# Two 1 KB reads of k and v put ahead of the first loads of a fused attention and channel-mix kernel

## The chip, the cores and the metric

The kernel runs on one core of one Trainium2 chip. The metric is the device time of one execution in microseconds (us). Unless a run says otherwise, a time is the median of its runs, with the lowest and highest behind it. The program uses a single core, so it has no second, slower die to compare against; the runs counted as fast are those within 1.5% of the fastest of the same kernel, and all comparisons use those.

## The reference

Eight batches of 8 heads, 576 positions, 64 features per head. A linear attention, then a channel mix whose input is the attention's output:

```python
def _attn_ref(q, k, v):
    q_s = np.exp(q - max over the last axis);  q_s = q_s / sum over the last axis
    k_s = np.exp(k - max over positions);      k_s = k_s / sum over positions
    kv = np.einsum('bhsd,bhse->bhde', k_s, v)
    return np.einsum('bhsd,bhde->bhse', q_s, kv)

def _moe_ref(x, mu_k, mu_r, w_k, w_v, w_r):
    xk = mu_k * x + (1.0 - mu_k) * x_prev        # x_prev: x one position earlier
    xr = mu_r * x + (1.0 - mu_r) * x_prev
    k = np.maximum(xk @ w_k, 0.0)
    return 1.0 / (1.0 + np.exp(-(xr @ w_r))) * (k * k @ w_v)
```

(Shortened: the maxima and sums are written in words, and the guards of 1e-09 and the casts are left out.)

## The kernel before

The kernel plans its instructions in advance: each operation is added to a plan with an engine, a cost and a key, and a scheduler emits them in the order of their planned start. What matters here is how batch 0 gets in. Six loads, q, k and v of head group 0 and then of group 1, each in two halves of 288 KB, fill the buffers raw_a to raw_f. The first load is issued by ACT, the other five by SP:

```python
PARTS = {1: [slice(0, 2)], 2: [slice(0, 1), slice(1, 2)]}
FIRST = ((0, 0, ("ACT", "ACT")), (0, 1, ("SP", "SP")), (0, 2, ("SP", "SP")),
         (1, 0, ("SP", "SP")), (1, 1, ("SP", "SP")), (1, 2, ("SP", "SP")))
# ... (cut)
        def emit(engine, u):
            ap = bass.AP(tensor=src.tensor,
                         offset=src.offset + (b * H + 2 * g + 4 * u.start) * S * D,
                         ap=[[J * D, 128], [4 * S * D, u.stop - u.start], [1, J * D]])
            return queues[engine].dma_start(out=raws[slot.index][:, u, :], in_=ap)
```

So raw_a is q of group 0, raw_b k, raw_c v, and raw_d, raw_e, raw_f the same of group 1. Two small loads of the mixing vectors stand ahead of SP's five:

```python
    def emit_mu_rows_load():
        for m, src in enumerate((moe_mu_k, moe_mu_r)):
            nc.sync.dma_start(out=mu_rows[:, m, :], in_=bass.AP(
                tensor=src.tensor, offset=src.offset, ap=[[256, 2], [1, 256]]))
# ... (cut)
    for op in plan.order():
        op.made = op.emit()
        if op.engine == "POOL" and op.size and gate:
            tc.add_manual_dep(op.made.ins, gate.pop().made.ins.name, sync)
```

ACT takes the exponential of q and k (eq_a, ek_a for group 0, eq_b, ek_b for group 1), POOL casts v of group 0 (vv_a) and then issues the later loads and the weights (wk, wr, wv). The built program gives the DMAs of SP and ACT eight semaphores (counters that a landing raises) in turn: in the trace of the kernel before, the first halves of raw_a and raw_d, the first and the ninth DMA, share one. A ninth DMA is held on its queue until the first has landed; this is invisible in the source and is what most of this document is about. "The turn" below is a DMA's place in this round of eight.

The softmax here doesn't subtract the row's maximum and nothing guards it: scores larger than these inputs give would overflow.

Of the kernel before, what the change touches and what calls it, by code (L numbers as in the profile page):

```python
# [12 lines left out]
F32 = mybir.dt.float32  # L13
# [195 lines left out]
def kernel(  # L209
# [14 lines left out]
    B, H, S, D = q.shape  # L224
# [16 lines left out]
    plan = Plan(pools, shared)  # L241

    const = ctx.enter_context(tc.tile_pool(name="const", bufs=1))
# [47 lines left out]
    pick = const.tile([2, 2, 64], F32, name="pick")  # L291
    mu_all = const.tile([128, 2, 2, 2, 128], F32, name="mu_all")
    warm = const.tile([1, 1], F32, name="warm")



    copies = {"ACT": nc.scalar.copy, "DVE": nc.vector.tensor_copy, "POOL": nc.gpsimd.tensor_copy}
    queues = {"SP": nc.sync, "ACT": nc.scalar, "POOL": nc.gpsimd}
# [44 lines left out]
    def emit_late_consts():  # L343
        for t in xbs:
            nc.vector.memset(t[:, :, 0:1], 0.0)

    zero = plan.add("DVE", 0.1, 0.15, -10, emit_warm_zero)
    plan.add("ACT", 1.55, 1.6, 3.5, emit_warm, [zero])
    identity = plan.add("POOL", 0.6, 0.8, -9.1, emit_identity)
# [74 lines left out]
    for h in range(2):  # L424
        wv_done.append(plan.add("POOL", 0.8, 0.8, LOADS.index(f"wv{h}"), lambda h=h: emit_wv(h), gate,
                                size=1200.0))
# [434 lines left out]
```

## Time and profile before

| | before |
|---|---|
| time, first three runs | 202.3 us (201.98 to 202.84) |
| span of the profiled execution | 200.2 us, clock 0.997 |
| raw_d's first half issued, landed | 3.63, 9.54 us |
| first half of eq_b starts | 9.56 us |
| first dense matmul with a record | 18.30 us (the record of the one before it is missing; its weight load starts at 17.88) |

The prediction below shows the busy line, the chain of waits and some short windows. The timeline of SP's queue in the kernel before (columns: start us, length us, engine, line, operation, output<-input, count):

```profile
1.46 0.83 SPq L310 DMA_DIRECT2D raw_b<-in_k_dram  x2
2.33 0.90 SPq L310 DMA_DIRECT2D raw_c<-in_v_dram  x2
3.63 0.82 SPq L310 DMA_DIRECT2D raw_d<-in_q_dram  x2
4.49 1.57 SPq L310 DMA_DIRECT2D raw_e<-in_k_dram  x2
```

raw_b and raw_c go out back to back. Between the end of raw_c's issue (3.23) and raw_d's there are 0.40 us with nothing: the ninth DMA waits for the first half of raw_a. The Trainium skill, "Perfetto Trace Analysis", section "DMA Instruction — HWDGE (DVE, Sync)", says that the start of such an instruction in a profile is the moment when its semaphores are satisfied, and that the movement of the data is not in its length. The trace agrees on both: raw_d's issue starts at 3.63, 0.02 us after raw_a landed, lasts 0.82 for two halves, and the data land 5.91 us after it.

The second view is a table of windows of the kernel before (window, length, five engines' busy time with counts, clock, DMA share, GB/s; a packet counts whole in the window in which it starts):

```profile
3.60:5.20 1.60, 1.28 (x2) 0.50 (x2) 0.85 (x2) 1.36 (x2) 0.00 (x0) 1.00 0.96 313
5.20:6.40 1.20, 0.76 (x1) 0.00 (x0) 1.20 (x4) 0.94 (x2) 0.00 (x0) 1.00 0.91 255
6.40:7.60 1.20, 0.37 (x10) 0.24 (x14) 1.03 (x2) 0.46 (x2) 0.89 (x1) 1.00 1.03 359
7.60:8.80 1.20, 0.58 (x36) 0.45 (x36) 0.00 (x0) 0.44 (x1) 1.13 (x3) 1.00 1.01 388
```

### The profile page before, as it was taken

The numbers are of one execution on the slowest core, as the hardware profiler recorded it, in microseconds if no ns is written. First come the engines' busy times: TensorE is split into PE (matmuls) and PEld (weight loads), VectorE is DVE, ScalarE is ACT, GpSimd is POOL, SyncE is SP. The second block draws the span as 40 slices with busy tenths as digits, with TensorE's granted clock in tenths as the row PEclk, the third lists the DMA queues.
The fourth block names the chain that finished last, engine by engine and source line by source line (L and its number), as shares of the span: only waits on it lengthen the run. The fifth ranks groups of instructions, "written<-read, shape, count | busy, mean of one in ns | idle before, by whom it ended". The sixth has DMA issues, their size and how long they took to land.

```text
span 200.2 us, 5314 instructions
## 1 busy us (share of the span) xinstructions
PE 183.6 (92%) x2147; PEld 96.6 (48%) x2171; DVE 160.6 (80%) x348; ACT 136.9 (68%) x212; POOL 40.7 (20%) x66
## 2 busy tenths in 40 slices
PE   2547999999999999999999999999999999999992
PEld 0234554545444555454476455455455544544761
DVE  2498469798999999999979999999998998432531
ACT  5494595998999799978559978946842662552440
POOL 1584365644354123411300000000000000000000
PEclk9999999999999999999999999999999999999998
DMA  6999999999999999993991220242042204402514
GB/s 196 348 277 227 281 256 352 391 398 412 388 403 405 403 405 362 398 378 110 262 365 47 54 56 0 52 111 51 3 100 62 52 3 105 105 0 54 118 41 105
DMA packets 15520, 40.72 MB, mean 203 GB/s; under 512 B 2300, under 2 KB 3592, under 8 KB 15496
## 3 DMA queue, kind: packets, MB, share of 16 engines
q0 software_dynamic: 7840, 27.40, 40.6%
q1 hardware_dynamic: 7208, 12.26, 21.4%
q10 hardware_dynamic: 448, 0.72, 1.2%
q8 instruction: 17, 0.28, 0.6%
q14 instruction: 7, 0.06, 0.1%
HBM read 33.56 MB, written 9.44 MB: 215 GB/s over the span
## 4 chain that ended last, share of the span: by engine, by line
PE 88%; DMA 4%; DVE 3%; issue 1%; ACT 1%; DVEq 0%
PE mm_c L766 10%; PE mm_a L722 10%; PE mm_d L722 9%; PE mm_d L766 8%; PE mm_a L766 7%; PE mm_c L722 7%; PE mm_b L766 6%; PE mm_b L722 6%; PE mm_b L756 6%; PE mm_d L756 4%; PE mm_c L756 3%; PE att_b L520 3%; PE mm_a L756 3%; DMA raw_d<-in_q_dram 3%; PE att_a L520 3%; PE att_b L507 2%
## 5 line engine op out<-in xcount | busy, mean ns | idle before, releaser
L722 PEld LDWEIGHTS <-wk 128*128 128x128 bf16 x320 | 35.4, 114 | 27.7 <-issue 2.2
L722 PE MATMUL mm_a<-xk,wk 128*128 128x512 bf16 (+1 forms) x96 | 24.2, 362 | 0.3 <-issue 0.2
L722 PE MATMUL mm_d<-xk,wk 128*128 128x512 bf16 (+1 forms) x87 | 22.4, 370 | 0.1
L766 PEld LDWEIGHTS <-k_b 128*128 128x128 bf16 x152 | 14.5, 98 | 15.7 <-issue 0.7
L756 PEld LDWEIGHTS <-xr 128*128 128x128 bf16 x144 | 13.9, 98 | 15.9
L766 PEld LDWEIGHTS <-k_a 128*128 128x128 bf16 x144 | 13.4, 97 | 15.5 <-issue 0.4
L722 PE MATMUL mm_c<-xk,wk 128*128 128x512 bf16 (+1 forms) x66 | 16.0, 358 | 0.4 <-issue 0.3
L722 PE MATMUL mm_b<-xk,wk 128*128 128x512 bf16 (+1 forms) x62 | 15.5, 352 | 0.2
L756 PE MATMUL mm_b<-wr_bf,xr 128*128 128x512 bf16 x50 | 13.3, 379 | 0.1
L766 PE MATMUL mm_c<-wv_bf,k_a 128*128 128x512 bf16 x46 | 12.1, 379 | 0.2 <-issue 0.2
L766 PE MATMUL mm_c<-wv_bf,k_b 128*128 128x512 bf16 x47 | 12.1, 379 | 0.2 <-issue 0.2
L761 ACT ACTIVATE th_a<-mm_b 128x512 f32<-128x512 f32 x12 | 7.1, 595 | 6.4 <-PE mm_b L756 4.9
L766 PE MATMUL mm_d<-wv_bf,k_b 128*128 128x512 bf16 x39 | 10.1, 379 | 0.2 <-issue 0.2
L766 PE MATMUL mm_b<-wv_bf,k_a 128*128 128x512 bf16 x38 | 10.0, 379 | 0.2 <-issue 0.2
L766 PE MATMUL mm_a<-wv_bf,k_b 128*128 128x512 bf16 (+1 forms) x39 | 9.4, 358 | 0.1
L756 PE MATMUL mm_d<-wr_bf,xr 128*128 128x512 bf16 x34 | 9.1, 379 | 0.1
L766 PE MATMUL mm_d<-wv_bf,k_a 128*128 128x512 bf16 x28 | 7.5, 379 | 0.4 <-issue 0.3
L710 DVE TENSOR_TENSOR k_a<-rel_b 128x512 bf16<-128x512 bf16 (+1 forms) x14 | 5.6, 398 | 2.8 <-ACT rel_b L706 2.8
L710 DVE TENSOR_TENSOR k_a<-rel_c 128x512 bf16<-128x512 bf16 (+1 forms) x13 | 5.1, 389 | 3.4 <-ACT rel_c L706 3.4
L761 ACT ACTIVATE th_b<-mm_c 128x512 f32<-128x512 f32 x6 | 3.7, 610 | 5.6 <-PE mm_c L756 4.7
L756 PE MATMUL mm_c<-wr_bf,xr 128*128 128x512 bf16 x28 | 7.2, 379 | 0.1
L756 PE MATMUL mm_a<-wr_bf,xr 128*128 128x512 bf16 x28 | 7.2, 379 | 0.0
(275 smaller groups left out, 416.7 us busy)
## 6 DMA issues: line engine op xcount, KB each, us to landing
out_dram<-ot_a SPq DMA_DIRECT2D x24, 128.0 KB, 3.8
out_dram<-ot_b SPq DMA_DIRECT2D x24, 128.0 KB, 3.0
out_dram<-ot_c SPq DMA_DIRECT2D x22, 128.0 KB, 2.8
raw_b<-in_k_dram POOLq DMA_DIRECT2D x3, 576.0 KB, 9.4
raw_c<-in_v_dram POOLq DMA_DIRECT2D x3, 576.0 KB, 8.9
raw_d<-in_q_dram POOLq DMA_DIRECT2D x3, 576.0 KB, 10.1
raw_a<-in_q_dram POOLq DMA_DIRECT2D x2, 576.0 KB, 10.5
raw_e<-in_k_dram POOLq DMA_DIRECT2D x2, 576.0 KB, 11.6
```

Source lines behind the costliest of these rows:

```text
L507: nc.tensor.transpose(out=transposed()[64 * u:64 * u + 64, hf, 64 * j:64 * j + 64], in_=qss[qs.index][r, j, 64 * u:64 * u + 64], identity= ...
L520: nc.tensor.matmul(bank(xp)[64 * hf:64 * hf + 64, u, at + c:at + e], lhsT=w[r, hf, :], rhs=qts[qt.index][r, hf, src:src + e - c], start=(n ...
L710: nc.vector.tensor_tensor(out=k2s[k2.index][:, fc, 0:n], in0=rels[rel.index][:, 0:n], in1=rels[rel.index][:, 0:n], op=ALU.mult)
L722: nc.tensor.matmul(bank(kf)[:, 0:n], lhsT=(w[:, h, u, fc % 4:F // 2:4] if split[ct // 2] else w[:, u, F // 2 * h + fc % 4:F // 2 * (h + 1) ...
L756: nc.tensor.matmul(bank(rps), lhsT=xs[1][:, ct, c:c + 128], rhs=wr_bf[:, ct // 2 + 2 * (ct % 2), :], start=(ct == 0), stop=(ct == CT - 1))
L761: nc.scalar.activation(out=ths[th.index][:], in_=bank(rps), func=ACT.Tanh, scale=0.5)
L766: nc.tensor.matmul(bank(vps)[:, 0:w], lhsT=k2s[k2.index][:, ft, 128 * m:128 * m + 128], rhs=wv_bf[:, ft, e:e + w], start=(ft == 0), stop=( ...
```

## The change

The intent: the first read of k and of v by each DMA engine is taken to be slow, and v's falls bare on the path at 4.5 to 6.4 us. Two reads of 16 rows of 64 bytes each, spread over all 16 engines, should pay that price early, while the queue is still ramping up. The data are never used.

```diff
+    touched = const.tile([16, 5, 16], F32, name="touched")
# ... (cut)
+    def touch(engine, i, src, step):
+
+        return queues[engine].dma_start(out=touched[:, i, :], in_=bass.AP(
+            tensor=src.tensor, offset=src.offset, ap=[[step, 16], [1, 16]]))
+
+    for i, src in enumerate((k, v)):
+        plan.add("SP", 0.36, 0.4, i - 700, lambda i=i, src=src: touch("SP", i, src, 8 * S),
+                 size=10.0)
     zero = plan.add("DVE", 0.1, 0.15, -10, emit_warm_zero)
```

PE, DVE and ACT keep their order to the instruction. On POOL the first half of vv_a moves ahead of two small products.

## The prediction

> **What bounds the kernel now.** I read the busy line and the slices of the page first, then the chain of waits, then a table of short windows over the start, then the SP queue's timeline.
>
> ```profile
> PE 183.6 (92%) x2147; PEld 96.6 (48%) x2171; DVE 160.6 (80%) x348; ACT 136.9 (68%) x212; POOL 40.7 (20%) x66
> ...
> PE   2547999999999999999999999999999999999992
> ...
> DMA  6999999999999999993991220242042204402514
> ...
> PE 88%; DMA 4%; DVE 3%; issue 1%; ACT 1%; DVEq 0%
> ```
>
> TensorE is busy 183.6 of 200.2 us and is at 90% or more in every slice from the fifth to the last but one. Each slice is 5 us. What it lacks lies in the first four slices (about 20 us) and in the last. In windows of 20 us PE is busy 9.74 us of the first 20, between 19.50 and 19.89 of each later 20 and 16.11 of the last 20.2. So the middle is set by TensorE and the engines that feed it, and a change of the start is worth only as much as it moves the first dense matmuls (first layer, 18.30 us) earlier.
>
> The chain of waits at the start (columns: start us, us, what):
>
> ```profile
> 0.74 2.87 DMA raw_a<-in_q_dram
> 3.61 0.02 issue
> 3.63 5.91 DMA raw_d<-in_q_dram
> 9.54 0.02 issue
> 9.56 0.69 ACT eq_b L454
> 10.25 0.02 issue
> 10.27 1.50 DVE rsum_b L467 x2
> ...
> 13.41 0.69 PE att_b L507 x27
> ```
>
> The end is reached through raw_d, the q of batch 0's second group: ACT waits for it until 9.54 us, DVE sums and scales, PE transposes at 13.41. The step from raw_a to raw_d at 3.61 is a queue wait, not data: the built program gives SP's and ACT's DMAs eight semaphores in turn, and a ninth DMA waits until the first has landed. raw_d, the ninth, waits for raw_a's first half. But what sets 9.54 is bandwidth: six half loads of 288 KB (q, k, v in halves) are ahead of raw_d's first half. So the question is how fast the DMA engines run from 1.7 to 9.5 us. Windows of 0.2 us (columns: window, length, five engines' busy time, clock, DMA share, GB/s):
>
> ```profile
> 4.20:4.40 0.20, 0.20 (x1) 0.18 (x1) 0.05 (x1) 0.13 (x2) 0.00 (x0) 1.00 0.99 380
> ...
> 4.60:4.80 0.20, 0.20 (x1) 0.00 (x0) 0.20 (x1) 0.20 (x1) 0.00 (x0) 1.00 0.77 196
> 4.80:5.00 0.20, 0.20 (x2) 0.00 (x0) 0.20 (x1) 0.20 (x1) 0.00 (x0) 1.00 0.86 207
> ...
> 5.40:5.60 0.20, 0.20 (x1) 0.00 (x0) 0.20 (x1) 0.14 (x1) 0.00 (x0) 1.00 0.65 161
> ...
> 6.40:6.60 0.20, 0.00 (x0) 0.00 (x0) 0.20 (x1) 0.20 (x1) 0.00 (x0) 1.00 0.98 369
> ```
>
> The engines count as busy and move half as much from 4.6 to 5.8 us. The packets say why: a 2304-byte packet normally takes 93 ns, but from 4.5 to 6.4 some 35 of them took between 200 and 1148 ns. The same is seen from 1.7 to 2.9, where raw_a's first packets took up to 715 ns; the first mu packet took 838. At 3.6, where k's first packets are recorded, there is one of 918 and otherwise 93. The slow stretch at 4.6 comes just where the first engines end k's first half and may reach ahead to v. My reading, an inference: an engine's first access to a tensor is slow; q's is bare, k's was made early behind raw_a's traffic and is mostly hidden, v's stands bare on the path. That is what the change aims at.
>
> **What the Trainium skill says.** "DMA: Bandwidth & Descriptors", section "Why a DMA increments its semaphore by 16 and not by 1": the number of engines is the largest divisor up to 16 of the slowest dimension on both sides, so a touch of 16 rows uses all 16. The two mu loads have two rows, and the trace shows only two late steps of each one's semaphore, which agrees. The same page, "Latency and other measured facts", puts a tiny transfer's HBM round trip at about 800 ns at least; the mu packet's 838 ns agrees. The same page, "Issuing engines are not separate DMA queues", says that DMAs from SP and ACT share the 16 engines; in the window 3.0 to 4.4 the trace has ACT's queue at 57% and SP's at 46% of the engines' time, which agrees. No page that I found gives a price for an engine's first access to a tensor, so that price comes from the trace alone.
>
> **The change part by part.** I compared the instruction order of the two built kernels. PE, DVE and ACT keep theirs to the instruction.
>
> *Added:* two issues at the head of SP's queue. SP's two mu issues start 0.43 and 0.29 us before what follows (0.74, 1.17, 1.46), so two more of that kind move everything behind them on SP by about 0.7 us at most: the mu loads to about 1.46 and 1.75, raw_b from 1.46 to about 2.1. The mu row matmul at 3.92 moves to perhaps 4.5; ACT's copy of it at 6.05 stands behind ek_a, so this costs nothing, or a tenth or two on an engine that then waits anyway.
>
> raw_b's data are not wanted before raw_a's are through: its first packet is recorded at 3.5 us, and issued at 2.1 it can begin at about 3.1 (raw_a needed 1.0 us from issue to first packet). Cost about 0. The bytes, 2 KB at some 390 GB/s, are nothing.
>
> *Moved, semaphores:* two more DMAs turn the ring of eight by two. raw_c, not raw_d, is now the load that waits for raw_a's first half, so it is issued at about 3.65 rather than 2.33, and raw_d about 0.85 later than now, at about 4.5. At 3.65 raw_a and raw_b, 1.18 MB together, are not through: by 4.4 us the trace has moved 0.82 MB. raw_c's first packet can start at about 4.7, and the 1.18 MB end at about 5.3, so there are 0.6 us to spare. Cost about 0, with little room.
>
> *Removed:* the bare stall. From 4.4 to 6.0 the engines moved 0.39 MB, 242 GB/s by the page's count; at 390 they would have moved 0.62. The missing 0.23 MB are 0.6 us; the ragged recovery to 6.4 adds 0.1 to 0.2. At most 0.8 us.
>
> *Given back at the start:* the touches' own first accesses now fall with raw_a's, 16 engines times two tensors, when the engines ramp up (68, 127, 115, 196, 300, 362 GB/s in windows of 0.2 us from 1.6). The slow packets there end one after another, some 20 in 0.9 us. If accesses are served so, raw_a may land 0.1 to 0.4 us later. I take 0.2.
>
> *Moved, POOL:* vv_a's first half is cast ahead of mu_all's two products (1.36 us together), not behind. Its second half, now ending at 9.49, may end near 10.1, and the load raw_g, issued at 10.58 after raw_d's second half, comes at about 10.2: still not later than now.
>
> *Sum:* raw_d lands 0.8 - 0.2 = 0.6 us earlier, at 8.9. Behind it ACT, DVE and PE are chains of fixed length up to 18.30. The weights follow: the last of wk's rows landed at 21.70 for a matmul at 22.76, 1.06 us of slack, and POOL's issues move about 0.4 earlier too. So most of the 0.6 us is kept, and I take 0.55 off 202.3: **201.75 us**, which I round to 201.7.
>
> **The rivals.** *First: the touch does nothing.* If the slow packets at 4.6 are not first accesses to v but traffic between queues, or the price goes by smaller pieces of a tensor than the 288 KB which the touch's rows span (they step 18 KB), the stall stays. For it: the slow packets fall among k's second half as well, 590 KB into k, and v's own packets are not marked. Against it: raw_e and raw_f, later and from untouched parts of the same k and v, run at 369 to 449 GB/s from 9.4 to 11.2 us. It would give 202.3 to 202.6. *Second: the stall only moves* ahead onto raw_a, and raw_c's new semaphore wait runs the queue dry. For it: the serial look of the ends at 1.9 to 2.9 and only 0.6 us to spare. It would give 202.2 to 202.8. *Third: more is gained than the stall*, because engines no longer drift apart (raw_d's semaphore steps are spread from 8.18 to 9.54 over engines) and all land near the earliest. This gives up to 1.2 us, about 201.1. *Fourth: POOL becomes the gate,* raw_g and the weights come no earlier, and the gain is cut to about 0.4: 201.9.
>
> **Range and chances.** Three runs of the kernel before span 0.86 us, so noise alone makes about 0.4 either way. The working case is 201.75, the third rival 201.1, the first two 202.3 to 202.8: I set 200.9 to 202.5. Two per cent is 4 us. The whole start up to raw_d is 9.5 us and the stall in it 0.8, so faster by over 2% would need a second gain five times the stall; slower would need a queue that hangs for 4 us. Each gets 0.01.
>
> **What will show it.** Right: the windows from 4.6 to 6.4 stay above 350 GB/s; raw_d's wait in the chain ends near 8.9 instead of 9.54, and the transposes of att_b and the first dense matmul move by 0.4 to 0.6 us; PE's 183.6 us stay. The ramp of the first windows after 1.6 us is slower than now if the price was moved there. Wrong: the dip at 4.6 is still there (first rival); a gap in SP's queue opens after 5 us and raw_a lands later (second); raw_d lands at 8.9 but the dense matmuls still start at 18.3 (POOL or the weights gate it). The size will be wrong if TensorE's slow first matmuls, 616 to 634 ns at 18.3 to 20.8 against 379 later, fall otherwise.

## The result, and the profile after

| | before | after |
|---|---|---|
| time, same rounds | 202.34 us (201.98 to 202.84, 4 runs) | 203.19 us (202.93 to 203.27, 4 runs) |
| ratio after / before | | 1.0038 [1.0015, 1.0062] |
| span of the profiled execution | 200.2 us | 201.5 us, clock 0.994 |

A ratio here and below is the mean time of one kernel's fast runs over the mean of the other's of the same rounds, with its 95% interval, so it is not quite the ratio of the medians quoted. By the 2% measure the kernels are the same. But the change is slower by 0.4%, where the prediction had it 0.3% faster, and 203.19 lies outside its range. The changed kernel was later measured twice more, five rounds each, beside new runs of the kernel before: 1.0081 and 1.0079.

The page of the changed kernel: busy line, two rows of slices of about 5 us, and the chain by engine:

```profile
PE 185.6 (92%) x2171; PEld 96.6 (48%) x2171; DVE 160.6 (80%) x348; ACT 136.8 (68%) x212; POOL 40.0 (20%) x66
...
PE   0538999999999999999989999999999999999991
...
DMA  5999999999999999993892220242042204402514
...
PE 84%; DMA 8%; DVE 4%; SPq 1%; ACT 0%; issue 0%; DVEq 0%
```

The 185.6 us of PE against 183.6 before are no extra work: the line counts 2171 matmuls against 2147, while both kernels have 2171 weight loads, so 24 records were missing in the trace before. What these lines show of the difference is at the start: the first slices read 0538 where they read 2547, and "SPq", the queue of SP, has come into the chain. The first dense weight load starts at 18.67 us, 0.79 later than before.

SP's queue in the changed kernel:

```profile
0.74 0.40 SPq L350 DMA_DIRECT2D touched<-in_k_dram  x1
1.20 0.41 SPq L350 DMA_DIRECT2D touched<-in_v_dram  x1
...
2.28 0.83 SPq L311 DMA_DIRECT2D raw_b<-in_k_dram  x2
3.73 0.80 SPq L311 DMA_DIRECT2D raw_c<-in_v_dram  x2
4.58 0.91 SPq L311 DMA_DIRECT2D raw_d<-in_q_dram  x2
5.53 1.22 SPq L311 DMA_DIRECT2D raw_e<-in_k_dram  x2
```

raw_b goes out 0.82 us later than before (2.28 for 1.46), raw_c 1.40 later (3.73 for 2.33), raw_d 0.95 later (4.58 for 3.63). Between raw_b and raw_c SP stands still for 0.62 us. The chain says what for (start us, us, what):

```profile
0.74 2.97 DMA raw_a<-in_q_dram
...
3.73 0.33 SPq L311
...
4.10 0.43 SPq L311
...
4.58 5.72 DMA raw_d<-in_q_dram
...
10.32 0.69 ACT eq_b L463
```

raw_a lands at 3.71, SP issues raw_c's two halves at 3.73 and 4.10, and only then raw_d, which lands at 10.30. Everything behind raw_d is as long as before: eq_b starts 0.76 us later than in the kernel before (10.32 for 9.56), its second half 0.79 later, and so do the instructions of ACT up to 20.9 us.

What the DMA engines did meanwhile, in the same windows as shown of before:

```profile
3.60:5.20 1.60, 0.65 (x1) 0.50 (x2) 0.75 (x2) 1.36 (x2) 0.00 (x0) 1.00 0.86 160
5.20:6.40 1.20, 1.20 (x2) 0.00 (x0) 1.20 (x5) 0.00 (x0) 0.00 (x0) 1.00 0.92 353
6.40:7.60 1.20, 0.52 (x7) 0.20 (x10) 1.07 (x2) 1.18 (x3) 0.00 (x0) 1.00 1.01 357
7.60:8.80 1.20, 0.62 (x34) 0.49 (x35) 0.00 (x0) 0.56 (x1) 0.00 (x0) 1.00 0.89 244
```

Multiply each last column by its length. From 3.6 to 5.2 us the changed kernel moved 160 x 1.6 = 256 KB where 313 x 1.6 = 501 were moved before, 245 KB less. From 5.2 to 6.4 it moved 118 KB more: the dip of before is gone from this place. From 6.4 to 7.6 both are equal. From 7.6 to 8.8 it moved 173 KB less, a second dip. The balance is 300 KB, at the 390 GB/s of an undisturbed stretch 0.77 us, which fits the 0.76 us by which raw_d came later. So the stall was not removed: it came earlier and deeper, and a second one came behind it.

Later in the run the rest of the difference of the spans (1.33 us in all) comes about in three steps. ACT's lag of 0.79 us shrinks to 0.46 at 21 to 24 us, where the first matmuls run slow for a shorter time, stays at 0.46 to 103 us, and is 0.95 from 105 us on. There one store is late; the waits of the changed kernel from 100 to 106 us (engine, line, what for, us in total, times, longest):

```profile
DVE ot_a L781 <- DMA out_dram<-ot_a: 1.9, 1, 1.9
...
PE mm_d L731 <- DVE ot_a L781: 0.4, 1, 0.4
```

Before, DVE's ot_a waited in the same place for PE, 1.5 us, and PE did not wait for it. This wait comes and goes among the kernels below (it is in the profiles of 1, 6, 7, 10, 13 and 15, not in those of 2, 14 and 16), so I count it as noise of single executions; why that store is late was not looked into.

The last 0.37 us lie behind the last store and are not noise. At its end SP waits for the eight semaphores one after another in a fixed order, about 0.06 us a wait. In the kernel before the last store has the last semaphore of that order. In the changed kernel the turn is two places on, the last store has the second, and six waits are still to come when it lands. No printed view shows this; it is worked out from the trace's records of landings and of SP's waits, and it is the same in every profile:

| turn | kernels | waits still to come | last landing to end, us |
|---|---|---|---|
| as before | the kernel before, 3, 5, 9, 11, 13, 15, 17, 18 | 0 | 0.90 to 0.91 |
| two places back | 4, 8, 10 | 2 | 1.03 |
| two places on | the change (three profiles), 1, 2 | 6 | 1.27 to 1.28 |
| one place on | 12 | 7 | 1.34 |

(In 7 and 14, also two places on, that landing has no record; from the end of DVE's last instruction to the end of the span they take 3.85 and 3.86 us, the changed kernel 3.87, the kernel before 3.49.) So the turn has a price at the end of the kernel that has nothing to do with its start.

### The profile page after: what moved, and what is told of

Same layout as the page of the kernel before. It is cut to its first block, busy times and chain, and to the rows that moved or that the text cites. A ratio compares the mean times of both kernels' runs of the same rounds, so it can differ in the third digit from the quotient of the medians.

```text
span 201.5 us, 5339 instructions
## 1 busy us (share of the span) xinstructions
PE 185.6 (92%) x2171; PEld 96.6 (48%) x2171; DVE 160.6 (80%) x348; ACT 136.8 (68%) x212; POOL 40.0 (20%) x66
## 4 chain that ended last, share of the span: by engine, by line
PE 84%; DMA 8%; DVE 4%; SPq 1%; ACT 0%; issue 0%; DVEq 0%
PE mm_c L775 10%; PE mm_a L731 9%; PE mm_d L731 9%; PE mm_d L775 7%; PE mm_c L731 7%; PE mm_a L775 7%; PE mm_b L775 6%; PE mm_b L731 6%; PE mm_b L765 5%; PE mm_d L765 4%; DMA out_dram<-ot_a 3%; PE mm_c L765 3%; DMA raw_d<-in_q_dram 3%; PE att_b L529 3%; PE mm_a L765 3%; PE att_a L529 2%
## 5 line engine op out<-in xcount | busy, mean ns | idle before, releaser
L775 PE MATMUL mm_d<-wv_bf,k_a 128*128 128x512 bf16 x32 | 8.2, 380 | 0.0
```

Source lines behind the costliest of these rows:

```text
L775: nc.tensor.matmul(bank(vps)[:, 0:w], lhsT=k2s[k2.index][:, ft, 128 * m:128 * m + 128], rhs=wv_bf[:, ft, e:e + w], start=(ft == 0), stop=( ...
```

## The experiments

All kernels keep the instruction order of the kernel before, frozen, except for what is named. They ran in groups of two to four (1 to 4, 5 to 8, 9 to 12, 13 to 16, 17 and 18), each group on one chip with its own runs of the kernel before. In experiments 3, 4, 9 and 13 the mixing vectors are a constant, which is wrong; the comparison let them pass. Two questions were open: is there a first access to k and v that a touch can pay for, and which of the three things that the two issues do (delay raw_b, turn the semaphores, read k and v) costs the time.

The edits share one helper in the final emission loop, printed once; the experiments differ in the place, the engine and the tensor:

```diff
-    for op in plan.order():
+    ordered = plan.order()
+
+    def touch(engine, i, src, rows, step):
+        queues[engine].dma_start(out=touched[0:rows, i, :], in_=bass.AP(
+            tensor=src.tensor, offset=src.offset, ap=[[step, rows], [1, 16]]))
+
+    for op in ordered:
```

**1. The order on POOL undone.** The touches stand ahead of the mu loads as in the change, everything else stays as before:

```diff
+        if op is rows_load:
+            touch("SP", 0, k, 16, 8 * S)
+            touch("SP", 1, v, 16, 8 * S)
```

> The changed kernel with every engine's order as in the kernel before; only the two touches are added at the head of the SP queue, so POOL casts vv_a after mu_all again. Theory A (delay: raw_b is issued 0.8 us later because two more issues stand ahead of it, and the touch itself does nothing): 203.1 us, ratio to the kernel before 1.003 to 1.005, raw_d ends near 10.3 us. Rival P (POOL's new order, which ends the second vv_a cast 1.5 us later, is what costs): back to 202.3, ratio 1.000 to 1.001.

Measured: 203.19 us (203.09 to 203.58), ratio 1.0061 [1.0007, 1.0115]; raw_d issued at 4.40, landed at 10.41. The loss is there without POOL's new order, so that order is not its cause.

**2. The same two reads, of q.** Neither k nor v is read early:

```diff
-            touch("SP", 0, k, 16, 8 * S)
-            touch("SP", 1, v, 16, 8 * S)
+            touch("SP", 0, q, 16, 8 * S)
+            touch("SP", 1, q, 16, 8 * S)
```

> As f1, but both touches read q, which raw_a opens anyway, so k and v are not touched; issues, queue and semaphores the same. Theory A: no difference from f1 (203.1). Rival T+ (touching k and v saves some of the stall, and the delay costs more than it): slower than f1 by 0.3 to 0.7 us, 203.5 to 203.9. Rival T- (the touches of k and v themselves disturb the loads): faster than f1, near 202.4.

Measured: 202.84 us (202.23 to 203.42), ratio 1.0040 [0.9982, 1.0098], an interval that holds 1; raw_d issued at 4.49, landed at 10.28. raw_d landed where it did with k and v touched (10.30, 10.41).

**3. The touches in place of the mu loads.** As many issues and as many places in the turn as before (wrong result):

```diff
-            nc.sync.dma_start(out=mu_rows[:, m, :], in_=bass.AP(
-                tensor=src.tensor, offset=src.offset, ap=[[256, 2], [1, 256]]))
+            nc.vector.memset(mu_rows[:, m, :], 0.5)
```

> The two touches stand in place of the two mu row loads, which are replaced by a constant fill on DVE (result wrong on purpose): raw_b is issued when it is in the kernel before, and the semaphores turn as before. The touch alone, without the delay. Theory A: 202.3, ratio 0.999 to 1.001, raw_d near 9.5 us and the dip of the DMA rate at 4.6 to 6.4 us still there. Rival T+: the dip gone, raw_d at 8.9, 201.7. Rival T-: 202.8 or more.

Measured: 202.61 us (201.26 to 202.84), ratio 1.0015 [0.9953, 1.0078]; raw_d issued at 3.72, landed at 9.97. The rate was 184 to 323 GB/s in the windows of 0.4 us from 3.6 to 6.0 us: k and v had been touched, and the dip was there. Because the interval is wide it was measured twice more (experiments 9 and 13).

**4. Neither touches nor mu loads on SP** (wrong result; the edit is the one of experiment 3 without the touches):

> No touches and no mu row loads on SP (constant fill, result wrong on purpose): raw_b is issued at 0.74 us instead of 1.46. Theory A (delay): the mirror image of the change, raw_d about 0.5 to 0.8 us earlier and 201.5 to 201.8, ratio 0.996 to 0.998. If the delay of raw_b is not the cause: 202.3, ratio 0.999 to 1.001.

Measured: 202.25 us (201.78 to 202.51), ratio 1.0005 [0.9940, 1.0070]. The windows are what this run was worth:

```profile
3.60:5.20 1.60, 0.15 (x1) 0.00 (x0) 0.00 (x0) 0.45 (x1) 0.00 (x0) 1.00 1.06 409
5.20:6.40 1.20, 0.00 (x0) 0.00 (x0) 0.75 (x1) 0.33 (x2) 0.00 (x0) 1.00 1.03 401
6.40:7.60 1.20, 0.00 (x0) 0.00 (x0) 0.58 (x1) 1.20 (x3) 0.00 (x0) 1.00 1.06 411
```

There is no dip at all, although nothing had touched k or v. So a first access to v does not cost a stall wherever it falls. (It could still be hidden behind other traffic; the packets of the touches themselves, below, speak against that.) eq_b started at 8.56 us, 1.0 earlier than before, but the time did not follow: raw_a landed later (its first exponential started 1.1 us later), ACT's copy of mu_all came 1.4 us later, POOL issued the next loads at 11.0 us, and the chain of waits now ran through POOL and the weights. An early raw_d is worth only as much as POOL's chain leaves.

**5. The kernel before again,** to see what a copy of itself measures:

> The kernel before, built again with nothing changed but a helper variable. It gives the floor of the noise: ratio 1.000, interval about 0.3% either way. Second profile of it: theory A (the start is decided by when raw_b is issued) expects raw_d's wait to end again within 0.2 us of 9.54 with a dip of the DMA rate after 4.5 us; if the start is mostly luck it lies anywhere from 8.9 to 10.3.

Measured: 201.88 us (201.07 to 202.80), ratio 1.0019 [0.9982, 1.0056]; raw_d issued at 3.74, landed at 9.08. By this interval the ratios are good to about 0.4% in one direction or the other. Those of one group share the runs of the kernel before, so those of 6 to 8 may all be up to 0.2% too high.

**6. The changed kernel again:**

> The changed kernel again, beside the kernel before on this chip. Theory A: ratio 1.003 to 1.005, raw_d's wait ends at 10.1 to 10.5. If the slowdown of the first measurement was luck: ratio 0.999 to 1.001.

Measured: 202.82 us (202.18 to 204.41), ratio 1.0081 [1.0035, 1.0128]; raw_d issued at 4.65, landed at 10.19. The loss is real.

**7. The touches between raw_b and raw_c.** raw_b is issued at 1.44 us, as before; only what comes after is delayed, and the turn is two places on:

```diff
+        if op is first[4]:
+            touch("SP", 0, k, 16, 8 * S)
+            touch("SP", 1, v, 16, 8 * S)
```

> The two touches stand between raw_b and raw_c: raw_b is issued at 1.46 us as in the kernel before, and only what the change does to the semaphores and to raw_c and raw_d stays (raw_c issued at 3.65). Theory A1 (late raw_b costs): raw_d near 9.5 to 9.7, ratio 0.999 to 1.001. Theory A2 (raw_c's new wait on raw_a costs): raw_d at 10.1 or later, ratio 1.003 to 1.005.

Measured: 202.96 us (201.71 to 203.40), ratio 1.0071 [1.0035, 1.0107]; raw_c issued at 3.73, raw_d at 4.59, and eq_b starts at 10.14. The delay of raw_b is not needed for the loss; two more DMAs in the turn ahead of raw_c are enough.

**8. raw_b first, mu on POOL's queue,** an attempt at a better kernel with a right result:

```diff
-            nc.sync.dma_start(out=mu_rows[:, m, :], in_=bass.AP(
+            nc.gpsimd.dma_start(out=mu_rows[:, m, :], in_=bass.AP(
+    ordered.remove(rows_load)
+    ordered.insert(ordered.index(identity) + 1, rows_load)
```

(and vv_a ahead of mu_all's products).

> No touches; the mu row loads go to POOL's queue, so raw_b is the first DMA of SP (0.74 us), and POOL casts vv_a before the mu products, so that raw_g is issued at about 10.0. Results right. Theory A1: the DMA rate has no dip (as when the mu loads were left out), raw_d's wait ends at 8.5 to 8.7, and since POOL no longer holds raw_g back the gain stays: ratio 0.994 to 0.997. If the start's gain is lost in the loads that follow: 0.998 to 1.001.

Measured: 202.38 us (202.18 to 202.90), ratio 1.0051 [1.0020, 1.0082], slower. Again no dip, 383 to 415 GB/s in windows of 0.5 us from 3 to 9 us. But the two mu rows, issued on POOL's queue at 1.47 and 2.14 us, landed 5.3 and 5.6 us later; the matmul and ACT's copy that need them came at 7.6 and 9.6 us, ahead of eq_b in ACT's order, and eq_b started at 10.70. One line of its chain:

```profile
2.14 5.27 DMA mu_rows<-in_moe_mu_r_dram
```

**9. The touches in place of the mu loads, five rounds:**

> The two touches in place of the two small mu loads on the same queue, mu set to a constant (wrong result on purpose), once more with five rounds: number of issues and places of the semaphore turn as in the kernel before. Theory of the issue times: raw_d issued near 3.7, lands at 9.1 to 10.0, ratio 0.999 to 1.002. If touching were harmful in itself (its 64-byte packets), 1.004 to 1.008; if it helped, 0.995 to 0.998 and no dip.

Measured: 201.71 us (201.24 to 203.01), ratio 0.9976 [0.9944, 1.0007], just below the 0.999 to 1.002 of no effect; but in its profiled execution, the slowest of its six, the rate was 290 to 323 GB/s in windows of 0.5 us from 3.5 to 6.0 us and raw_d's second half landed at 11.13. Undecided at this point.

**10. raw_b and raw_c merged, no touch.** Each is one DMA of 576 KB; two issues and two places in the turn fewer:

```diff
+    merged = {(0, 0, 1): None, (0, 0, 2): None}
+            if merged.get((b, g, i)):
+                return merged[b, g, i]
+            if (b, g, i) in merged:
+                u = slice(0, 2)
```

> The kernel before with raw_b and raw_c each issued as one DMA of 576 KB in place of two of 288 KB: two issues fewer ahead of raw_d and two places of the semaphore turn back, so the opposite of the change. Theory of the issue times (a load lands about 5.3 to 6.3 us after its issue, and the later it is issued the more slow packets it meets): raw_c is issued near 1.9 us, raw_d near 2.5 to 2.9 without a wait, its first half lands at 8.5 to 8.9 instead of 9.1 to 9.5, no dip in the DMA rate from 4 to 6 us, ratio 0.995 to 0.999. Rival (the dip belongs to k's second half and v's first half whatever the time of issue): dip stays at 4.5 to 6 us, raw_d lands at 9.1 to 9.5, ratio 0.999 to 1.002. Rival (finer loads let the casts begin earlier, so merging costs): ek_a starts later by 0.3 us or more and the ratio is over 1.002.

Measured: 202.80 us (201.92 to 203.35), ratio 1.0018 [0.9989, 1.0047]. A miss: raw_d was issued at 2.40 us, 1.2 earlier than before, and landed at 10.14, 7.7 us later. The rate was 263 to 360 GB/s in windows of 0.5 us from 3.5 to 7.5 us. So an earlier issue does not by itself bring an earlier landing, and my theory that a load lands 5.3 to 6.3 us after its issue holds only around the issue times of before and after.

**11. Merged, with the touches at the head of SP.** raw_b is delayed as in the change, but raw_d, not raw_c, is the one that waits for raw_a:

> The change, with raw_b and raw_c each issued as one DMA: the two touches are there and delay raw_b by 0.8 us, but the two places of the semaphore turn are given back, so raw_d again waits for raw_a's first half as before. Theory that the place in the semaphore turn carries the loss (raw_c and raw_d issued too late): raw_c is issued near 3.2 us, raw_d near 3.7, it lands at 9.1 to 9.8, ratio 0.999 to 1.002. Rival (the delay of raw_b by the two issues carries it): raw_d lands at 10 or later and the ratio is 1.004 to 1.008 as with the change.

Measured: 202.60 us (201.44 to 203.32), ratio 1.0008 [0.9975, 1.0042]; raw_d issued at 3.52, landed at 9.14. With the turn given back, most of the loss is gone although raw_b is issued at 2.29 us. (The profiled execution was the fastest of the six.)

**12. One touch.** Only v, at the head of SP: half the delay, half the turn:

```diff
+        if op is rows_load:
+            touch("SP", 0, v, 16, 8 * S)
```

> Half the dose: only the touch of v at the head. Theory of the issue times: raw_b is issued 0.4 us later, raw_c's second half waits for raw_a's first half, raw_d is issued near 4.1 us and lands at 9.5 to 10.0, ratio 1.001 to 1.004. The reading on record (v's first access is the stall and k's touch is of no use): the dip is gone, raw_d lands at 9.0 or earlier, ratio 0.996 to 1.000.

Measured: 202.93 us (202.40 to 203.58), ratio 1.0024 [0.9992, 1.0056]; eq_b started at 10.28. It lies between no turn and the whole turn, and the dip is not gone (196 to 286 GB/s in windows of 0.5 us from 3.5 to 5.5 us), but the interval reaches 1. The end of the kernel alone accounts for 0.43 us of its time.

At twelve runs two things were open: the delay and the turn had been told apart only through merged loads, with intervals that overlapped, and the touch in itself had measured 1.0015 and 0.9976.

**13. The touches in place of the mu loads, a third time:**

> The touches in place of the two mu loads once more (wrong result on purpose), because its two measurements, 1.0015 and 0.9976, lie on both sides of 1. Theory (the touch neither helps nor harms): 0.998 to 1.002. The reading on record (the touch is worth 0.6 us): 0.995 to 0.998 again, and a first half of eq_b before 9.0 us.

Measured: 201.57 us (200.79 to 203.18), ratio 0.9997 [0.9960, 1.0033]; eq_b at 9.46. The three together, 1.0015, 0.9976 and 0.9997, have a mean of 0.9996: no effect.

**14. The turn alone.** Two reads of q on ACT's queue behind raw_a, where ACT has nothing to do yet. SP issues nothing more, raw_b goes out at 1.45, but raw_c is held:

```diff
+        if op is first[1]:
+            for i in range(2):
+                touch("ACT", i, q, 16, 8 * S)
```

> The semaphore turn alone: two 1 KB reads of q (neither k nor v) issued on ACT's queue behind raw_a, where ACT is free; nothing is added on SP, mu and raw_b are issued when they were, but the turn of eight is two places on, so raw_c's first half waits for raw_a's first half. Theory (raw_c and raw_d held by the turn is what costs): raw_b issued at 1.46, raw_c near 3.7, raw_d near 4.6, raw_d lands at 10.0 to 10.4, eq_b's first half starts 10.0 or later, ratio 1.003 to 1.008 like the change. Rival (raw_b's delay by two issues on SP, or the touching of k and v, costs): ratio 0.999 to 1.002.

Measured: 202.90 us (202.06 to 203.44), ratio 1.0062 [1.0034, 1.0089]. The time is what the theory expected. The profile is not: the profiled execution was the fastest of the six, raw_c was issued at 3.7 and landed 3.3 us later, eq_b started at 9.34, and its chain of waits runs another way:

```profile
1.16 4.33 DMA raw_a<-in_q_dram
5.49 0.02 issue
5.52 0.68 ACT eq_a L455
...
7.34 1.69 POOL mu_all L376 x2
...
12.50 8.47 DMA wk<-in_moe_w_k_dram
```

Here raw_a's second half landed at 5.49 us and POOL's chain to the weights was the long one. So this run shows that the turn costs time, 0.37 us of it at the end of the kernel, not that it costs the rest through raw_d in every execution; the slower five have no profile.

**15. The touches of k and v alone.** Issued on ACT's queue, raw_b and raw_c merged so that the turn stands as before, right result:

```diff
+        if op is first[1]:
+            touch("ACT", 0, k, 16, 8 * S)
+            touch("ACT", 1, v, 16, 8 * S)
```

> The touches of k and v alone, with a right result: issued on ACT's queue behind raw_a, raw_b and raw_c each merged into one DMA so that the turn stands as before (raw_d waits for raw_a's first half) and nothing is added on SP. Theory (the turn costs, the touch neither helps nor harms): raw_d issued near 3.7, lands at 9.0 to 9.6, ratio 0.998 to 1.002. The reading on record (touching takes the stall away): no window of 0.5 us under 350 GB/s from 3 to 8 us, raw_d lands at 8.9 or earlier, ratio 0.995 to 0.998. If touching harms in itself: 1.004 or more.

Measured: 201.28 us (200.56 to 202.25), ratio 0.9978 [0.9949, 1.0007]; raw_d issued at 3.68, landed at 9.22, and the dip was in place, though k and v had been touched:

```profile
3.60:5.20 1.60, 1.57 (x2) 0.49 (x2) 0.50 (x1) 1.59 (x4) 0.00 (x0) 1.00 1.05 392
5.20:6.40 1.20, 0.47 (x1) 0.00 (x0) 1.20 (x5) 0.10 (x1) 0.00 (x0) 1.00 0.81 241
```

Its interval and that of the turn alone do not overlap, with the same two issues on the same queue. (The loads are merged in one and not in the other; experiment 10, merged without any extra DMA, at 1.0018 gives no sign that merging alone makes it faster.)

**16. The changed kernel on the same chip:**

> The changed kernel itself, on the same chip, as the measure for the turn alone. 1.004 to 1.008 as in its two earlier measurements, raw_d landing at 10.0 to 10.4.

Measured: 203.14 us (202.84 to 204.64), ratio 1.0079 [1.0047, 1.0110]; raw_d issued at 4.64, eq_b at 10.06. The turn alone, at 1.0062, accounts for most of it; the difference of the two is within their intervals.

**17 and 18. Experiment 15 with q in place of k and v, and experiment 15 again:**

> The kernel of e3_merge_act with its two touches reading q instead of k and v: same issues, same turn, nothing of k or v read early. Theory (touching k and v is worth nothing): the same as e3_merge_act within 0.3 per cent, 0.996 to 1.001, raw_d lands at 9.0 to 9.6. The reading on record (a first access to v is the stall): 0.4 per cent slower than e3_merge_act, with a deeper dip between 4.5 and 6.5 us.

> e3_merge_act again, to see whether it holds as a version that beats the kernel before: 0.995 to 0.999 if its 0.9978 was real, 0.999 to 1.001 if it was chance.

Measured: with q 201.77 us (200.60 to 202.42), ratio 0.9964 [0.9928, 1.0000]; with k and v 202.01 us (201.39 to 202.93), ratio 0.9990 [0.9959, 1.0021]. Touching k and v is not better than touching q, rather worse by chance. This form, merged loads and two placeholder reads on ACT, has three ratios below 1, but each interval reaches 1 and the k and v one fell back to 0.999; I do not call it a kernel that beats the one before. But 17 is the closest partner of 14, with the same two reads of q on ACT's queue: 1.0062 [1.0034, 1.0089] with the turn two places on, 0.9964 [0.9928, 1.0000] with merged loads that give the two places back. Merged loads with the turn two places on were not tried.

**All kernels together.** "Held" means that raw_c waits for raw_a.

| | ratios |
|---|---|
| raw_c held: the change (three times), 1, 2, 7, 14 | 1.0038, 1.0081, 1.0079, 1.0061, 1.0040, 1.0071, 1.0062 |
| half of raw_c held: 12 | 1.0024 |
| raw_c not held: 3, 9, 13, 4, 5, 10, 11, 15, 18, 17 | 1.0015, 0.9976, 0.9997, 1.0005, 1.0019, 1.0018, 1.0008, 0.9978, 0.9990, 0.9964 |
| mu late: 8 | 1.0051 |

The means of the first and third row are 1.0062 and 0.9997, and no kernel of one row lies among the other. Delay on SP and tensor touched are mixed in both rows; the new order on POOL is in the first row alone (and is not needed there: 1), merged loads in the third alone. The first row also has the longer end of the kernel. So of its 0.62%, about 1.25 us, 0.37 us come from the end and some 0.9 are left for the rest of the kernel; the table cannot tell whether these come through the hold on raw_c or another effect of the same turn.

The start of eq_b in the profiled execution goes with its time as well. Of the 18 kernels with a profile other than experiments 4 and 8, whose chains run elsewhere, six have eq_b before 9.6 us, with times of 200.56 to 202.06, and twelve at 9.9 us or later, with 202.10 to 203.39. But the same kernel can fall on either side: experiments 9 and 13 are one kernel, with eq_b at 10.40 and 9.46 and 203.01 and 200.79 us. So the stalls vary from execution to execution by about as much as the change costs; the turn moves the odds, and all three profiles of the changed kernel (10.32, 10.22, 10.06) are on the late side, both of the kernel before (9.56, 9.11) on the early one.

## Why the prediction was wrong

The direction and the size were wrong within the 2% class; the chances of 0.01, 0.98, 0.01 held. By its own steps:

- **"Removed: the bare stall", at most 0.8 us: the step that failed.** The cause put under it, an engine's first access to v, is refuted. With k and v touched the dip stayed (3, 12, 15) and moved (the change), without any touch it was absent (4, 8), and with q touched nothing differed (2; 17 against 18). The prediction's own first rival had the argument for it: slow packets fell 590 KB into k. The packets of the touches say it most directly: all 32 took 8 to 11 ns each in the changed kernel, k's at 1.75 to 2.25 us and v's at 2.85 to 3.3, so there was no price of a first access for them to pay. Yet of the first 37 packets of raw_b, whose tensor k had been touched, 18 took 0.24 to 1.21 us. What a slow packet waits for was not found.
- **"Moved, semaphores: cost about 0, with little room": failed too, and it is where the loss comes from.** The times of issue were right: raw_c expected at 3.65, measured 3.73; raw_d at 4.5, measured 4.58. The reasoning, that a load issued while 1.18 MB are still to come cannot be missed, was not: 300 KB less were moved by 8.8 us, and raw_d came 0.76 us later. And the step looked at the start alone: the two places also put six more waits behind the last store, 0.37 us. Kernels with this turn measured 1.0062 on average, about 1.25 us of 201.7, both together.
- **"Added: cost about 0": about right.** raw_b went out at 2.28, expected 2.1. With this delay and no turn the ratio was 1.0008 (11), and with the turn and no delay 1.0071 and 1.0062 (7, 14).
- **"Given back at the start", 0.2 us: at most 0.1.** raw_a landed at 3.71, 3.79 and 3.78 us in the changed kernel, at 3.61 and 3.73 in the kernel before, and the cause given for it, slow first accesses of the touches, was not there.
- **"Moved, POOL": not the cause (1),** but its time was wrong: raw_g was issued at 11.37, not 10.2, behind raw_d's second half at 11.07.
- **The sum** had raw_d at 8.9; it landed at 10.30. Of these 1.4 us, 0.6 are the gain that was not there and 0.76 the loss against before. The second rival, that the stall moves ahead and raw_c's wait hurts, was the right one in kind, with 202.2 to 202.8; in size it fell short by 0.4, about what the end of the kernel adds.
- **Readings to correct.** From 4.5 to 6.4 us 26 packets took over 200 ns, not some 35. Of the four packets of the mu loads only the first took 838 ns; the others took 46 to 62.

What stays open: why late issue and slow packets go together. Taken over all engines it is not a shortage of bytes asked for: raw_a and raw_b are 1.18 MB, and by the end of the first dip of the changed kernel, at 5.2 us, 0.77 MB had been moved (the sum of the trace's packets). (Some engines may have been through with their share; the DMA share of 0.86 in that window leaves room for it.) And it is not issue time alone, since experiment 10 issued raw_d earliest and got it late. Nor is it the depth of the first dip: from 3.6 to 5.2 us the change moved 160 GB/s and experiment 7 385, with the same loss. One thing sets the two kernels without a dip (4, 8) apart: raw_b is SP's first DMA, with nothing small ahead of it, and its packets start at 1.75 us beside raw_a's; in all other profiles SP's first large packet starts between 3.2 and 3.9 us. Whether the small DMAs ahead or the time of issue make this difference was not tested.

## What to carry to other kernels

A DMA that is tiny in bytes is not tiny in a queue: it takes 0.4 us of issue and a place in whatever turn the semaphores take, and those that pay are the load that now waits two places earlier and, here, the end of the kernel. Before adding one, list which DMA each issue is held by, before and after, and where the last store comes in the round. And when a stall is put down to a cause such as a first access, test the cause with a read of something else before building on it.

## What the Trainium skill lacked or had wrong

- No page that I found has the turn: SP's and ACT's DMAs share eight semaphores in this build, and a ninth waits for the first. Here raw_c was held from 3.11 us, when raw_b's issue ended, to 3.73, and kernels with that turn measured 1.0062 on average.
- No page that I found has the waits at the end: SP goes through these semaphores in a fixed order, about 0.06 us each, and the time from the last store's landing to the end was 0.90 to 1.34 us by the place of its semaphore.
- "DMA: Bandwidth & Descriptors", section "Issuing engines are not separate DMA queues", calls the time on the sequencer to initiate a DMA "usually small relative to the DMA itself". A 1 KB read took 0.40 us of SP's queue and 1.8 to 2.7 us from issue to landing, which agrees; what the sentence leaves out is that this time and the place in the turn fall on the loads behind, here 0.95 us on raw_d's issue.
- "DMA: Bandwidth & Descriptors", section "Anatomy of one DMA — SWDGE (gpsimd) path", puts the fixed cost of one DMA at about 2.0 us. Two 2 KB loads on POOL's queue, beside 288 KB loads of other queues, took 5.3 and 5.6 us from issue to landing (experiment 8). Their packets took 46 ns each and the first started at 5.61 us, so the difference is waiting, for which that section has no term.
- No page that I found prices the slow packets at the start, 0.2 to 1.2 us where 93 ns is usual, and the runs here did not find their cause.
